# Experts' dot products on TensorE for every other tile, the gate product on GpSimd, filler products in the first chunk

## The chip, the cores and the metric

The kernel runs on one core of a Trainium2 chip. Its time is the device time of one execution in microseconds; the kernel before took 851.04 us (median of three runs, 850.98 to 857.43). TensorE multiplies matrices into PSUM; VectorE (DVE), ScalarE (ACT) and GpSimd (POOL) work on elements; SyncE (SP) issues nearly all transfers. Each engine works through its own queue in order and waits at semaphores for the others.

## The reference

Three layers in float32 follow each other.

```python
# 1. gated linear attention, 4 batches x 8 heads x 768 positions, head size 40, step by step:
m_new = maximum(f_gate[t] + m, i_gate[t])
f_stab, i_stab = exp(f_gate[t] + m - m_new), exp(i_gate[t] - m_new)
C = f_stab * C + i_stab * outer(v[t], k[t]);  n = f_stab * n + i_stab * k[t]
y[t] = sigmoid(o_gate[t]) * (C @ q[t]) / maximum(abs(n @ q[t]), 1)
# 2. on the 3072 rows of 320: h = x @ w_in (320 x 2048);  x = (h - tanh(h)) @ w_out
# 3. eight experts, one for each row:
logits = normalize(x) @ normalize(expert_emb).T / tau
e = argmax(logits);  gate = softmax(logits)[e]
out = gate * (relu(x @ w1[e]) @ w2[e])          # 320 -> 1024 -> 320
```

## The kernel before, in words

The 768 positions are cut into six **chunks** of 128; with four batches a chunk has four **units** (chunk `c`, batch `b`, unit `i = 4c + b`) of eight heads. Attention of a unit is made of pieces (in `attention`): `scores` (S: products of q and k into PSUM, exponentials on ScalarE, a mask on GpSimd), `weigh` (W: mask times scores on VectorE, and k times the last column of the mask), `outs` (O: on TensorE the state products `po`, the state's update `st`, and eight weighted sums `pi`, one for each head), `sums` (M: denominators, the **gate product** `z` = sigmoid times reciprocal, and the state `Cst`, scaled by the decay `eGL` and added to), `finish` (F: y = sum times z), `turn` (U: y transposed on TensorE) and `low` (L: the transposed rows as a high and a low part). From chunk 2 on q and k are split into high and low parts first (`parts`, Q).

The first layer's products (second in the reference) run in 96 **steps**, 16 for each chunk of 512 rows. A step is 8 TensorE products of 512 columns (`gemm1`, into `h`), a chain ScalarE, VectorE, ScalarE, GpSimd (`g_chain`, `g_split`) and 12 products of 320 columns (`gemm2`, into four `acc` banks). `gemm1` runs three steps ahead. While chunk `c` runs through its steps, the attention of chunk `c + 1` and the **routing** of chunk `c - 1` are woven in: `PLACE1` and `PLACE2` say at which step and position a piece stands, `ORDER` the positions within a step ('g' the special pieces and gemm2, 'r' one portion of routing, 'h' gemm1, the digits the attention pieces). In the first 16 steps the weights of this layer are prepared too (`prep`), and in chunk 5 the experts' weights begin.

Routing (`route`, `slots`) takes a chunk's result as four tiles of 128 rows, and makes for each tile the sums of squares and the eight dot products with the experts' normalized vectors. `VDOT[c]` says how many of the eight are made on VectorE (L263, a product with a running sum); the rest are a product on GpSimd (L267) and a sum on ScalarE (L268). Where `VDOT` is 0, as for chunk 5, `dots` makes them on TensorE: three transposes of the tile, two copies out of PSUM, three products with the transposed vectors `enT`, one copy of 8 columns. `enT` is made by `turn_en` at step 96 - 6 = 90. Then come exponentials, each row's place in its expert's list, and scatters to `xs`. Behind the 96 steps the experts' stage reads `xs` and runs 80 shorter steps.

What stands ahead of the bar in `START` (the **start**) runs in the order written there; chunk 0 has its attention there, in the letters above. What is traced after that is put in order by the framework's planner, which takes the traced order as priority and moves an instruction behind others when, by its own cost estimates, its inputs or its buffer come later. `at_bank` gives out PSUM banks; in the steps there are two of them for all of attention and routing, in turn.

`warm` issues filler products of 512 bf16 columns whose result nobody reads: `WARM0` = 20 at the very start, and two ahead of every scores piece of chunk 0.

Of the kernel before, what the change touches and what calls it, by code (L numbers as in the profile page):

```python
# [9 lines left out]
F32 = mybir.dt.float32  # L10
# [5 lines left out]
AF = mybir.ActivationFunctionType  # L16
ALU = mybir.AluOpType
# [5 lines left out]
NCH = S // L  # L23
# [4 lines left out]
E = 8  # L28
# [25 lines left out]
STACK = 12  # L54
SIGM = (2, 14)
EXPERT_X = (-3, 0)
LOAD_EW, LOAD_X, LOAD_X2, TURN_EN = 13, 4, 4, 6
KW_POOL = (0, 2, 3, 4, 5)
VDOT = (8, 8, 8, 8, 6, 0)
WARM0, WARM = 20, 2  # L60


BETA, GAMMA, C2 = -1.2788614, 4.7605257, 0.052115805
# [47 lines left out]
def build(ctx, tc, qk, qk3, vk, og, gat, w64, w12, emb, tau, cst, tok, empty, out):  # L111
    nc = tc.nc
    V, A, G, T = nc.vector, nc.scalar, nc.gpsimd, nc.tensor
    MM = T.matmul

    const = ctx.enter_context(tc.tile_pool(name="const", bufs=1))
# [105 lines left out]
    enT = []  # L222

    def turn_en():

        e8 = attp.tile([8, 320], F32, tag="z", name="e8", bufs=1)
        nc.sync.dma_start(out=e8, in_=es)
        pn = at_bank("pn")
        enT.append(attp.tile([128, 3, 8], F32, tag="dn", name="enT"))
        for k in range(3):  # L230
            n = min(128, 320 - 128 * k)
            T.transpose(pn[0:n, 8 * k:8 * k + 8], e8[:, 128 * k:128 * k + n], ident[0:8, 0:8])
            A.activation(out=enT[0][0:n, k, :], in_=pn[0:n, 8 * k:8 * k + 8], func=AF.Copy)

    def dots(x2, lg):

        pd = at_bank("pd")
        xt = attp.tile([128, 384], F32, tag="y", name="xt")
        for k in range(3):
            n = min(128, 320 - 128 * k)  # L240
            T.transpose(pd[0:n, 128 * k:128 * k + 128], x2[:, 128 * k:128 * k + n], ident)
        V.tensor_copy(out=xt[:, 0:256], in_=pd[:, 0:256])
        A.activation(out=xt[0:64, 256:384], in_=pd[0:64, 256:384], func=AF.Copy)
        for k in range(3):
            n = min(128, 320 - 128 * k)
            MM(pd[:, 384:392], xt[0:n, 128 * k:128 * k + 128], enT[0][0:n, k, :], start=k == 0, stop=k == 2)
        V.tensor_copy(out=lg, in_=pd[:, 384:392])

    def slots(pool, nj, R, si, vdot=E, part=E):

        n = nj * 8
# [3 lines left out]
        for j in range(nj):  # L255
            x2 = R[:, j, 0:320]
            A.activation(out=jk[0], in_=x2, func=AF.Square, accum_out=ss[:, j:j + 1])
            if vdot == 0:
                dots(x2, lg[:, j, :])
                yield  # L260
            for e in range(E if vdot else 0):
                if e < vdot:
                    V.scalar_tensor_tensor(out=jk[1], in0=x2, scalar=1.0, in1=enb[:, e, :], op0=ALU.mult, op1=ALU.mult,  # L263
                                           accum_out=lg[:, j, e:e + 1])
                else:
                    dt = attp.tile([128, 320], F32, tag="A", name="dt")
                    G.tensor_tensor(out=dt, in0=x2, in1=enb[:, e, :], op=ALU.mult)  # L267
                    A.activation(out=jk[0], in_=dt, func=AF.Copy, accum_out=lg[:, j, e:e + 1])  # L268
                if (e + 1) % part == 0:
                    yield  # L270
# [20 lines left out]
        for j in range(1, nj):  # L291
# [12 lines left out]
                        in1=col(C_EOFF, n).rearrange("p (j e) -> p j e", j=nj), op=ALU.add)  # L304
# [67 lines left out]
    attp = p1.enter_context(tc.tile_pool(name="attp", bufs=2))  # L372
# [3 lines left out]
    Cst = attp.tile([104, 16, 82], F32, tag="C", name="C", bufs=1)  # L376
    gts = {}
    units = {}
    sig = {}
# [3 lines left out]
    eGL = attp.tile([104, NCH * 16], F32, tag="eGL", name="eGL", bufs=1)  # L383
# [143 lines left out]
    def attention(c):  # L527
# [3 lines left out]
        def unit(b):  # L531
            i = c * B + b
# [50 lines left out]
            def outs():  # L583
                po = v['po'] = at_bank("po")
                st = po[:, 336:500].rearrange("p (j d) -> p j d", j=4)
                if i >= TWO:
                    for h in range(8):
                        MM(po[:, 42 * h:42 * h + 42], v['q', h % 2][0:120, h // 2 * L:(h // 2 + 1) * L],
                           C3[0][0:120, b, h % 2, h // 2, :], start=True, stop=True)
                elif c:  # L590
                    for j in range(4):
                        MM(po[:, 82 * j:82 * j + 82], qT[0:104, j, :], Cst[:, 4 * b + j, :], start=True, stop=True)
                if c + 1 < NCH:
                    for h in range(8):
                        p0 = 64 * (h % 2)
                        MM(st[p0:p0 + 40, h // 2, :], v['kw'][:, h, :], v1[:, h, :], start=True, stop=True)
                pi = v['pi'] = at_bank("pi")
                for h in range(8):
                    MM(pi[:, 41 * h:41 * h + 41], v['A', h % 2][:, h // 2, :], v1[:, h, :], start=True, stop=True)
                if i >= 4:  # L600
                    load_d(i + 2)
                if 4 <= i < TWO - 2:
                    load_unit(i + 2)
                elif 4 <= i < NCH * B - 2:
                    units[i + 2] = load_vk(i + 2)
                if TWO - 2 <= i < TWO:
                    load_half(i + TWO + 2)

            def sums():
# [5 lines left out]
                if c:  # L615
                    Tt = v['T'] = attp.tile([128, 8, 41], F32, tag="T", name="T", bufs=1)
                    V.tensor_tensor(out=tmp, in0=po[:, 0:w * 8].rearrange("p (h d) -> p h d", h=8)[:, :, 0:41],
                                    in1=eG[:, 8 * i:8 * i + 8].unsqueeze(2).to_broadcast([128, 8, 41]),
                                    op=ALU.mult)
                    V.tensor_tensor(out=Tt.rearrange("p h d -> p (h d)"), in0=pi[:, 0:328],  # L620
                                    in1=tmp.rearrange("p h d -> p (h d)"), op=ALU.add)
                else:
# [4 lines left out]
                V.tensor_tensor(out=dn, in0=nq, in1=dn, op=ALU.max)  # L627
                V.reciprocal(out=dn, in_=dn)
                z = v['z'] = attp.tile([128, 8, 40], F32, tag="z", name="z", bufs=1)
                (V if c > 1 else G).tensor_tensor(out=z, in0=sig[i].rearrange("p (h d) -> p h d", h=8),  # L630
                                                  in1=dn.to_broadcast([128, 8, 40]), op=ALU.mult)
                if c == 0:
                    for par in range(2):
                        p0, c0 = 64 * par, 41 * par
                        A.activation(out=Cst[p0:p0 + 40, 4 * b:4 * b + 4, c0:c0 + 41], in_=st[p0:p0 + 40, :, :],
                                     func=AF.Copy)
                for par in range(2 if 0 < c < NCH - 1 else 0):
                    p0, c0 = 64 * par, 41 * par
                    Cv = Cst[p0:p0 + 40, 4 * b:4 * b + 4, c0:c0 + 41]
                    V.tensor_tensor(out=Cv, in0=Cv, in1=eGL[p0:p0 + 40, 4 * i:4 * i + 4].unsqueeze(2)  # L640
                                    .to_broadcast([40, 4, 41]), op=ALU.mult)
                    V.tensor_tensor(out=Cv, in0=Cv, in1=st[p0:p0 + 40, :, :], op=ALU.add)
            def finish():
                y = v['y'] = attp.tile([128, 384], F32, tag="y", name="y")
# [139 lines left out]
    def warm(bank, n=None):  # L784
        for _ in range((WARM if c0[0] else 0) if n is None else n):
            MM(bank, oneb, busy, start=True, stop=True)
# [30 lines left out]
    NS = NCH * NF  # L817
# [136 lines left out]
            sp[n] = relu_chain(hs.pop(n), rows_of(step(n)[0])[3])  # L954

    def special(n, c, f, rx):
        if n == NS - TURN_EN:
            turn_en()
        if n == NS - NF - 4:
            ranking()  # L960
# [274 lines left out]
```

## Time and profile before

| | |
|---|---|
| median of three runs | 851.04 us (850.98 to 857.43) |
| profiled execution | 854.08 us, span 852.1 us |
| TensorE busy | 763.0 us (90%) |
| VectorE busy | 638.1 us (75%) |
| ScalarE busy | 496.1 us (58%) |
| GpSimd busy | 364.3 us (43%) |
| mean granted TensorE clock | 0.927 |

The span is that of one profiled execution, from its first to its last instruction. Busy time is the time in which an engine works on an instruction; TensorE's matmuls are pipelined and their ends are modelled, so that a busy TensorE is not one at its peak. The clock is the share of 2.4 GHz that was granted: 1.00 or, in some stretches, 0.50. A row's idle time and its releaser say how long the engine had nothing to do ahead of it and what came last. The first `gemm2` of each chunk marks the chunks: they begin at 73.4, 176.3, 275.5, 374.3, 463.8 and 545.7 us, and the experts' stage at 621.7.

### The profile page before, as it was taken

Reading aid. Unit: us, or ns where it says so; the run is one execution under the profiler, and the core shown is the slowest. Engines: PE = TensorE matmul, PEld = TensorE weight load, DVE = VectorE, ACT = ScalarE, POOL = GpSimd, SP = SyncE. Lnnn points to the kernel's source line nnn. Section 1 sums busy time; section 2 is a strip of 40 time slices with the busy share of each in tenths; the row PEclk is TensorE's granted clock in tenths of the full one; section 3 lists DMA queues with packets and bytes.
Section 4 is the critical chain, followed back from the end, with each engine's and each line's share of the span. In section 5 each row is a group of like instructions: output and inputs, shape, how many; then the busy total and the mean of one; then the engine's idle time right before and its main releaser. Section 6 shows DMA issues by size and latency. Waiting matters only on the chain. (4 is left out here: it accounts for less than half of the span.)

```text
span 852.1 us, 14301 instructions
## 1 busy us (share of the span) xinstructions
PE 763.0 (90%) x4640; PEld 677.6 (80%) x4640; DVE 638.1 (75%) x1417; ACT 496.1 (58%) x1175; POOL 364.3 (43%) x375
## 2 busy tenths in 40 slices
PE   8979899797899898998889989888899999999994
PEld 5767778686788687787778778767799989999994
DVE  6476999898887989879986999797473775556420
ACT  3775787767557645685558634655554655455421
POOL 2383677657463554655463525443522111012111
PEclk8558998988989989999999999999999999999998
DMA  8574766543344243432335311201535764455000
GB/s 273 211 254 160 257 220 198 133 122 93 87 126 131 82 101 87 143 105 79 89 109 152 92 34 44 73 1 51 177 115 164 232 181 140 120 173 165 36 20 21
DMA packets 60756, 107.55 MB, mean 126 GB/s; under 512 B 24958, under 2 KB 33321, under 8 KB 60016
## 3 DMA queue, kind: packets, MB, share of 16 engines
q1 hardware_dynamic: 57968, 98.46, 38.8%
q0 software_dynamic: 2512, 7.89, 2.5%
q8 instruction: 38, 0.62, 0.3%
q14 instruction: 46, 0.38, 0.1%
q10 hardware_dynamic: 192, 0.20, 0.1%
HBM read 92.91 MB, written 17.87 MB: 130 GB/s over the span
## 5 line engine op out<-in xcount | busy, mean ns | idle before, releaser
L185 PE MATMUL h<-xh,wi 128*128 128x512 f32 (+6 forms) x880 | 303.3, 382 | 18.8 <-DVE g L213 13.3
L185 PEld LDWEIGHTS h<-xh,wi 128*128 128x128 f32 x880 | 171.7, 198 | 45.7 <-DVE g L213 17.3
L193 PE MATMUL acc<-wo,ghi 128*128 128x320 f32 (+1 forms) x616 | 200.6, 326 | 0.0
L162 POOL TENSOR_TENSOR glo<-g,ghi 128x512 fp32r<-128x512 f32 x96 | 133.2, 1389 | 156.6 <-ACT ghi L218 119.8
L185 PE MATMUL h<-xl,wi 128*128 128x512 f32 (+6 forms) x528 | 197.7, 379 | 0.4
L195 PE MATMUL acc<-wo,glo 128*128 128x320 f32 (+1 forms) x616 | 194.9, 317 | 2.0 <-POOL glo L162 2.0
L194 PE MATMUL acc<-wo,ghi 128*128 128x320 f32 (+1 forms) x616 | 194.7, 316 | 0.0
L218 ACT ACTIVATE ghi<-g 128x512 fp32r<-128x512 f32 x96 | 60.2, 628 | 111.7 <-DVE g L213 94.6
L193 PEld LDWEIGHTS acc<-wo,ghi 128*128 128x128 f32 (+1 forms) x616 | 118.4, 192 | 6.1 <-ACT D L568 1.3
L195 PEld LDWEIGHTS acc<-wo,glo 128*128 128x128 f32 (+1 forms) x616 | 117.7, 191 | 4.0 <-POOL glo L162 3.2
L194 PEld LDWEIGHTS acc<-wo,ghi 128*128 128x128 f32 (+1 forms) x616 | 118.1, 192 | 3.2
L185 PEld LDWEIGHTS h<-xl,wi 128*128 128x128 f32 x528 | 105.0, 199 | 12.3 <-DVE xl L660 1.6
L212 DVE SCALAR_TENSOR_TENSOR s<-s,u 128x512 f32<-128x512 f32 x96 | 78.9, 822 | 41.8 <-ACT s L211 40.2
L263 DVE SCALAR_TENSOR_TENSOR jk<-R,enb 128x320 bf16<-128x320 f32 x152 | 96.5, 635 | 2.7 <-ACT R L727 1.7
L156 POOL DMA_INDIRECT out<-ob,ti x29 | 28.5, 982 | 156.9 <-ACT ob L1053 133.3
L929 DVE SCALAR_TENSOR_TENSOR glo<-h,ghi 128x256 fp32r<-128x256 f32 (+5 forms) x80 | 41.4, 517 | 60.0 <-ACT ghi L928 54.5
L568 ACT ACTIVATE D<-D,bcol 128x128 f32<-128x128 f32 x192 | 64.6, 390 | 33.6 <-DMA D<-gd 33.3
L928 ACT ACTIVATE ghi<-h 128x256 fp32r<-128x256 f32 (+5 forms) x80 | 36.7, 458 | 65.4 <-PE acc L194 55.9
L162 DVE TENSOR_TENSOR wi<-ew,wi 128x256 fp32r<-128x256 f32 (+1 forms) x128 | 50.1, 392 | 31.4 <-ACT wi L174 29.8
L211 ACT ACTIVATE s<-u,cs 128x512 f32<-128x512 f32 x96 | 68.7, 716 | 0.9
L213 DVE SCALAR_TENSOR_TENSOR g<-s,h 128x512 f32<-128x512 f32 x96 | 65.4, 682 | 2.9
L210 ACT ACTIVATE u<-h 128x512 f32<-128x512 f32 x96 | 55.9, 583 | 12.6 <-PE h L185 11.3
(192 smaller groups left out, 1199.5 us busy)
## 6 DMA issues: line engine op xcount, KB each, us to landing
ew<-in_w SPq DMA_DIRECT2D x64, 352.0 KB
W<-in_qk SPq DMA_DIRECT2D x32, 480.0 KB
D<-gd SPq DMA_DIRECT2D x48, 256.0 KB
raw<-in_w SPq DMA_DIRECT2D x16, 704.0 KB
vk<-in_vk SPq DMA_DIRECT2D x20, 324.0 KB
xs<-blank SPq DMA_DIRECT2D x32, 161.0 KB
sg<-in_og SPq DMA_DIRECT2D x6, 640.0 KB
ys<-y SPq DMA_DIRECT2D x24, 160.0 KB
```

The lines of the kernel that those rows point to most:

```text
L162: eng.tensor_tensor(out=out, in0=x, in1=hi.bitcast(F32), op=ALU.subtract)
L185: MM(h[:, 0:cols], wi[:, k, :], x[:, kk, :], start=n == 0, stop=n == len(seq) - 1)
L193: MM(o, ghi[:, sl], wo[:, 0, 0:320], start=first, stop=False)
L194: MM(o, ghi[:, sl], wo[:, 1, 0:320], start=False, stop=False)
L195: MM(o, glo[:, sl], wo[:, 0, 0:320], start=False, stop=last)
L210: A.activation(out=u, in_=h, func=AF.Square, accum_out=usum[:, n:n + 1])
L211: A.activation(out=s, in_=u, func=AF.Square, bias=col(C_BETA))
L212: V.scalar_tensor_tensor(out=s, in0=s, scalar=GAMMA, in1=u, op0=ALU.add, op1=ALU.mult)
L213: V.scalar_tensor_tensor(out=g, in0=s, scalar=C2, in1=h, op0=ALU.mult, op1=ALU.mult)
L218: A.activation(out=ghi, in_=g, func=AF.Copy)
L263: V.scalar_tensor_tensor(out=jk[1], in0=x2, scalar=1.0, in1=enb[:, e, :], op0=ALU.mult, op1=ALU.mult, accum_out=lg[:, j, e:e + 1])
L568: A.activation(out=Dt[:, j, :], in_=Dt[:, j, :], func=AF.Exp, bias=bcol[:, k:k + 1])
```

## The change

- `slots`: in the routing of chunks 0 to 4, tiles 0 and 2 now take the path through `dots`, tiles 1 and 3 make all eight products on VectorE (`VDOT` 8 in place of 6 for chunk 4). Each `dots` tile is one portion of routing, each VectorE tile two.
- `dots`: the wide copy out of PSUM is on ScalarE.
- `turn_en` runs at step 12, and `enT` has a tile of its own.
- `outs`: in chunk 0 one filler stands ahead of each of the eight weighted sums of a unit, 32 in all. `WARM0` is 26.
- `sums`: the gate product is on GpSimd in every chunk (before, on VectorE from chunk 2 on). The decay of the state is one product over 104 partitions and 4 x 82 columns instead of two over 40 partitions and 4 x 41.

```diff
--- before.py
+++ after.py
@@ -54,10 +54,10 @@
 STACK = 12
 SIGM = (2, 14)
 EXPERT_X = (-3, 0)
-LOAD_EW, LOAD_X, LOAD_X2, TURN_EN = 13, 4, 4, 6
+LOAD_EW, LOAD_X, LOAD_X2, TURN_EN = 13, 4, 4, 12
 KW_POOL = (0, 2, 3, 4, 5)
-VDOT = (8, 8, 8, 8, 6, 0)
-WARM0, WARM = 20, 2
+VDOT = (8, 8, 8, 8, 8, 0)
+WARM0, WARM = 26, 2
 
 
 BETA, GAMMA, C2 = -1.2788614, 4.7605257, 0.052115805
@@ -226,7 +226,7 @@
         e8 = attp.tile([8, 320], F32, tag="z", name="e8", bufs=1)
         nc.sync.dma_start(out=e8, in_=es)
         pn = at_bank("pn")
-        enT.append(attp.tile([128, 3, 8], F32, tag="dn", name="enT"))
+        enT.append(const.tile([128, 3, 8], F32, tag="enT", name="enT"))
         for k in range(3):
             n = min(128, 320 - 128 * k)
             T.transpose(pn[0:n, 8 * k:8 * k + 8], e8[:, 128 * k:128 * k + n], ident[0:8, 0:8])
@@ -239,7 +239,7 @@
         for k in range(3):
             n = min(128, 320 - 128 * k)
             T.transpose(pd[0:n, 128 * k:128 * k + 128], x2[:, 128 * k:128 * k + n], ident)
-        V.tensor_copy(out=xt[:, 0:256], in_=pd[:, 0:256])
+        A.activation(out=xt[:, 0:256], in_=pd[:, 0:256], func=AF.Copy)
         A.activation(out=xt[0:64, 256:384], in_=pd[0:64, 256:384], func=AF.Copy)
         for k in range(3):
             n = min(128, 320 - 128 * k)
@@ -255,10 +255,11 @@
         for j in range(nj):
             x2 = R[:, j, 0:320]
             A.activation(out=jk[0], in_=x2, func=AF.Square, accum_out=ss[:, j:j + 1])
-            if vdot == 0:
+            on_pe = vdot == 0 or part < E and j % 2 == 0
+            if on_pe:
                 dots(x2, lg[:, j, :])
                 yield
-            for e in range(E if vdot else 0):
+            for e in range(0 if on_pe else E):
                 if e < vdot:
                     V.scalar_tensor_tensor(out=jk[1], in0=x2, scalar=1.0, in1=enb[:, e, :], op0=ALU.mult, op1=ALU.mult,
                                            accum_out=lg[:, j, e:e + 1])
@@ -596,6 +597,8 @@
                         MM(st[p0:p0 + 40, h // 2, :], v['kw'][:, h, :], v1[:, h, :], start=True, stop=True)
                 pi = v['pi'] = at_bank("pi")
                 for h in range(8):
+                    if c == 0:
+                        warm(idle, 1)
                     MM(pi[:, 41 * h:41 * h + 41], v['A', h % 2][:, h // 2, :], v1[:, h, :], start=True, stop=True)
                 if i >= 4:
                     load_d(i + 2)
@@ -627,18 +630,19 @@
                 V.tensor_tensor(out=dn, in0=nq, in1=dn, op=ALU.max)
                 V.reciprocal(out=dn, in_=dn)
                 z = v['z'] = attp.tile([128, 8, 40], F32, tag="z", name="z", bufs=1)
-                (V if c > 1 else G).tensor_tensor(out=z, in0=sig[i].rearrange("p (h d) -> p h d", h=8),
+                G.tensor_tensor(out=z, in0=sig[i].rearrange("p (h d) -> p h d", h=8),
                                                   in1=dn.to_broadcast([128, 8, 40]), op=ALU.mult)
                 if c == 0:
                     for par in range(2):
                         p0, c0 = 64 * par, 41 * par
                         A.activation(out=Cst[p0:p0 + 40, 4 * b:4 * b + 4, c0:c0 + 41], in_=st[p0:p0 + 40, :, :],
                                      func=AF.Copy)
+                if 0 < c < NCH - 1:
+                    Cu = Cst[:, 4 * b:4 * b + 4, :]
+                    V.tensor_tensor(out=Cu, in0=Cu, in1=eGL[:, 4 * i:4 * i + 4].unsqueeze(2).to_broadcast([104, 4, 82]), op=ALU.mult)
                 for par in range(2 if 0 < c < NCH - 1 else 0):
                     p0, c0 = 64 * par, 41 * par
                     Cv = Cst[p0:p0 + 40, 4 * b:4 * b + 4, c0:c0 + 41]
-                    V.tensor_tensor(out=Cv, in0=Cv, in1=eGL[p0:p0 + 40, 4 * i:4 * i + 4].unsqueeze(2)
-                                    .to_broadcast([40, 4, 41]), op=ALU.mult)
                     V.tensor_tensor(out=Cv, in0=Cv, in1=st[p0:p0 + 40, :, :], op=ALU.add)
             def finish():
                 y = v['y'] = attp.tile([128, 384], F32, tag="y", name="y")
@@ -954,7 +958,7 @@
             sp[n] = relu_chain(hs.pop(n), rows_of(step(n)[0])[3])
 
     def special(n, c, f, rx):
-        if n == NS - TURN_EN:
+        if n == TURN_EN:
             turn_en()
         if n == NS - NF - 4:
             ranking()
```

## Rows read from the trace of the kernel before

**Rows 1.** The page: granted TensorE clock in 40 slices of the span, in tenths.
```profile
PEclk8558998988989989999999999999999999999998
```
**Rows 2.** Windows, one a chunk: stretch, length, busy PE, PEld, DVE, ACT, POOL; clock.
```profile
73.40:176.30 102.90, 91.04 (x563) 79.44 (x562) 93.29 (x144) 73.69 (x168) 69.85 (x70) 0.91 0.57 181
176.30:275.50 99.20, 85.67 (x528) 75.71 (x527) 81.39 (x187) 62.02 (x149) 54.20 (x52) 0.91 0.44 119
275.50:374.30 98.80, 86.40 (x527) 76.14 (x526) 86.45 (x201) 61.19 (x143) 51.98 (x51) 0.91 0.37 100
374.30:463.80 89.50, 80.19 (x511) 70.24 (x510) 79.71 (x174) 57.96 (x136) 46.23 (x45) 0.98 0.40 111
463.80:545.70 81.90, 73.45 (x432) 63.73 (x431) 74.27 (x184) 44.67 (x107) 36.00 (x29) 1.00 0.22 68
545.70:621.70 76.00, 64.30 (x339) 54.84 (x339) 59.64 (x142) 46.19 (x122) 33.67 (x31) 0.96 0.22 69
```
**Rows 3.** TensorE's waits in chunk 1 (176 to 275 us): total, times, longest.
```profile
PE ps L564 <- DVE q L162: 9.3, 2, 5.3
```
**Rows 4.** Windows of three single steps: without attention, with weighted sums, in chunk 4.
```profile
482.10:485.80 3.70, 3.70 (x23) 3.33 (x23) 3.70 (x10) 2.29 (x4) 1.92 (x2) 1.00 0.34 90
362.30:369.10 6.80, 6.80 (x62) 6.32 (x60) 2.18 (x5) 6.77 (x14) 2.57 (x2) 1.00 0.39 94
518.90:525.20 6.30, 6.30 (x47) 5.93 (x46) 4.98 (x12) 3.42 (x8) 3.56 (x3) 1.00 0.08 29
```
**Rows 5.** Groups by line and shape: count, busy us, mean ns, idle before.
```profile
L263 DVE SCALAR_TENSOR_TENSOR jk<-R,enb 128x320 bf16<-128x320 f32 x152 | 96.5, 635 | 2.7 <-ACT R L727 1.7
...
L640 DVE TENSOR_TENSOR C<-C,eGL 40x164 f32<-40x164 f32 x32 | 17.3, 540 | 5.8 <-PE po L592 4.7 <-POOL Cl L162 0.6
...
L630 DVE TENSOR_TENSOR z<-sg,dn 128x320 f32<-128x320 f32 x16 | 12.7, 795 | 0.2
```
**Rows 6.** Timeline of TensorE in the last chunk's dots: start, length, instruction, count.
```profile
621.15 0.81 PE L241 MATMUL pd<-cs,R 128*128 128x128 f32 x6
...
622.84 0.93 PE L246 MATMUL pd<-enT,xt 128*128 128x8 f32 x6
```
**Rows 7.** Instructions on the tile pd: shortest, median, longest ns; first and last start.
```profile
L242 DVE COPY xt<-pd x4: 414/415/424, 621.7 to 626.1; 128x256 f32<-128x256 f32 x4
L243 ACT ACTIVATE xt<-pd x4: 266/270/271, 622.5 to 626.6; 64x128 f32<-64x128 f32 x4
```
**Rows 8.** Timeline, chunk 4: one small VectorE operation and the GpSimd products beside it.
```profile
527.26 2.89 DVE L627 TENSOR_TENSOR dn<-T,dn 128x8 f32<-128x8 f32 x1
...
527.56 2.56 POOL L162 TENSOR_TENSOR glo<-g,ghi 128x512 fp32r<-128x512 f32 x2
```
**Rows 9.** Timeline of TensorE in the start; in brackets idle time and releaser.
```profile
13.95 1.82 PE L562 MATMUL ps<-ue 40*128 40x128 f32 x8 [1.18 <-DMA ue<-in_qk]
...
20.58 3.64 PE L599 MATMUL pi<-ue,A 128*128 128x41 f32 x16
24.01 1.05 PE L786 MATMUL ps<-busy,oneb 128*128 128x512 bf16 x2
25.00 2.07 PE L562 MATMUL ps<-ue 40*128 40x128 f32 x8
...
41.56 0.77 PE L596 MATMUL po<-ue,kw 128*40 128x41 f32 x14 [0.30 <-POOL kw L578]
...
55.97 0.66 PE L653 MATMUL px<-cs,y 128*128 128x128 f32 x2 [4.25 <-DVE y L645]
...
67.30 1.86 PE L599 MATMUL pi<-vk,A 128*128 128x41 f32 x14
```
**Rows 10.** Window of the stretch that holds the dots of chunk 4's tiles.
```profile
544.00:575.00 31.00, 24.80 (x122) 20.61 (x120) 30.61 (x72) 19.80 (x59) 16.62 (x15) 0.94 0.00 1
```
**Rows 11.** Waits of the whole execution: GpSimd's mask for ScalarE's exponential.
```profile
POOL D L569 <- ACT D L568: 45.2, 23, 9.8
```
**Rows 12.** TensorE's waits in chunk 0 (73 to 176 us).
```profile
PE px L653 <- DVE y L645: 4.7, 2, 2.7
```

## Prediction

> **What bounds it now.** I read the page's busy shares and clock line first, then busy time chunk by chunk, then who TensorE waits for, then single rows. TensorE's clock is at half speed through much of the first 64 us and near full from there [rows 1]; the expert stage behind 621.7 us is touched by no part of the change. So the question is the start (to 73.4 us) and the six chunks of 16 steps each, 548.3 us together. In the chunks TensorE is busy for 481 us and VectorE for 475, the six rows added up [rows 2]: two engines, each nearly full, and neither covers the other. Who is the waiter? In chunk 1 TensorE's longest waits are for VectorE, its split of q above all [rows 3].
>
> What would TensorE need alone? A step with nothing beside the two products takes 3.7 us, one with a unit's weighted sums 6.8, and 6.3 in chunk 4, whose last units have no state product; TensorE is busy throughout and at full clock in all three [rows 4]. So 16 x 3.7 + 4 x 3.1 = 71.6 us is the floor of a chunk (69.6 in chunk 4); scores and transposes, alike in chunks 1 to 4, are left in what lies above. Above it stand 27.6 us in chunk 1, 27.2 in chunk 2, 17.9 in chunk 3, 12.3 in chunk 4. Chunk 4 carries the same products with the dots of chunk 3 on VectorE, but less state work. Its 12.3 us is the least excess that this schedule has shown, so I take it as what stays. Chunks 1 and 2 can then give back about 15 us each, chunk 3 5.6.
>
> **Part by part.** *Dots.* For chunks 0 to 3, 16 of the 32 dot products (two tiles of eight) leave VectorE; at 0.635 us [rows 5] that is 10.2 us a chunk, spent in the steps of the next chunk. For chunk 4 24 become 16: 5.1 us, and GpSimd's eight products with their eight sums on ScalarE go too. In their place comes, per tile, what the last chunk does already: three transposes, two copies, three products (each shows as two), a copy of 8 columns. Six transposes (two tiles) lasted 0.81 us and six product rows (one tile) 0.93 [rows 6]: at most 0.4 + 0.9 = 1.3 us of TensorE a tile, 2.6 a chunk, 13 over ten tiles. The wide copy moves from VectorE (0.415) to ScalarE, beside the narrow one of 0.27 [rows 7], so some 0.7 us a tile on an engine that is busy for 45 to 62 us in chunks 1 to 5 [rows 2]: nothing. If that cover fails, the products wait on TensorE with the next product of the chunk queued behind them; the rows show 0.88 us between the end of the transposes (621.96) and the first product (622.84), filled with other products. Uncovered it is 10 x 0.9 = 9 us; I take 0.
>
> *Gate product.* 16 products move from VectorE (0.795 each, 12.7 in all) to GpSimd [rows 5], four in each of chunks 1 to 4: 3.2 us a chunk. But VectorE and GpSimd hinder each other: an operation on 128 x 8 elements lasted 2.89 us while two GpSimd products ran for 2.56 [rows 8]. So the relief is between 0 and 3.2 a chunk; nearest is the mixed mean of all those rows, and I take half, 1.6.
> The Trainium skill's SBUF — State Buffer, "Who interferes with whom", says that a VectorE instruction with two SBUF inputs and a GpSimd one that reads SBUF lock each other out for a whole instruction, and by that rule the move would be worth the low end, nothing, 3.2 us less over chunks 1 and 2.
>
> *State decay.* Two products of 164 columns (0.540 each) become one of 328. Not seen before: between one half (0.54) and both (1.08); nearest is the gate product, 320 columns from SBUF, 0.795 [rows 5]. That saves 0.3 a unit, 1.1 us in each of chunks 0 to 3.
>
> *Experts' vectors turned at step 12 instead of 90*, in a tile of their own: three transposes, three copies and a small load on SP's queue move from chunk 5 into chunk 0, where TensorE idles 11.9 us [rows 2]. Nothing. The load needs the single buffer of the gate product, so loads behind it on SP could slip by a step, 6.4 us (102.9 / 16), once; I take 0. The new score banks and the turned tiles use buffers that attention uses (two each): 0 again, with the 9 us above as bound.
>
> *Fillers.* Unit 0's 16 sum products at half clock last 3.64 us; at full clock 14 of them last 1.86, so 2.1 for 16 [rows 9]. A pair of fillers takes 0.99 at half clock (24.01 to 25.00): eight are 4.0 us a unit, 2.0 at full. If the clock stays at half, four units add 16 us, less the 0.30 that TensorE waits at 41.56. If it rises in the first unit, each unit is 4.1 long, 0.5 more than now, and each scores piece (2.07 at half) loses about 1, but units 2 and 3 still wait for GpSimd at 41.56: about -1 in all. Between these no row decides: half-speed stretches there hold two fillers in some 3 us, and none holds eight. I take a rise with the second unit: 4.0 + 3 x 0.5 - 2 x 1.0 - 0.3 = +3. All of it reaches the end of the start, since the last unit's turn waited 4.25 us for VectorE behind these sums. The six extra fillers at the very start last at most 6 x 0.5 = 3.0, in part inside the 1.18 us that TensorE waited for a load at 13.95 [rows 9], and the first sums wait for GpSimd anyway: 0, at most 1.8.
>
> **The sum.** VectorE is relieved by 10.2 + 1.6 + 1.1 = 12.9 us in each of chunks 1 to 3. Chunks 1 and 2: 12.9 is below the 15 they can give, less 2.6 of TensorE: 10.3 each. Chunk 3: 5.6 - 2.6 = 3.0. Chunk 4: it is its own yardstick, 0. Chunk 5: its first 31 us hold the dots, and VectorE is busy for 30.6 of them [rows 10]: 5.1 - 2.6 = 2.5. Chunk 0: 1.1. Together 27.2, less 3 for the start: 24. The profiled execution took 854.08 us (span 852.1 and 2.0 outside it): 830. The median of the three runs is 3.04 lower: **827 us**.
>
> Bounds: all of the gate product's relief gives 3 more; at full clock instead of 0.91, TensorE's 172 us in chunks 1 and 2 would shrink by up to 15, since it was fewer waits, not less work, that chunk 4 had at clock 1.00; so some 809. The other way, 9 us of uncovered dots, 13 more of fillers: 849.
>
> **Rivals.**
> *A, VectorE was not what held the chunks.* For it: chunk 5 has the least VectorE work (59.6 of 76 us) and the highest idle share of TensorE, 11.7 of 76 [rows 2]; the chain of one step through ScalarE, VectorE and GpSimd waits for itself. Against it: 6.2 of that idle time lies in the 31 us of dots [rows 10], and chunks 2 and 4 rank in excess as in VectorE's load. Then dots only fill TensorE's holes, gains and costs cancel: 851 - 1 + 3 = 853, down to 843 if half remains. Chance 0.19.
> *B, the gate product comes late on GpSimd (slower).* GpSimd works in order and waits, 23 times, 2.0 us on average for a ScalarE exponential ahead of its masks, at worst 9.8 [rows 11]. A gate product queued behind that holds y, then y's transposes on TensorE, then every product behind. In chunk 0, where it is on GpSimd today, the transposes waited 4.7 us for y [rows 12], 1.2 a unit. At that price 16 units cost 19 us: 846. At 2.0 and its own 0.8 each they cost 45: 872. It turns the sign from 1.5 us a unit on. Against: the planner may put it ahead of the masks. Chance of slower by this 0.13.
> *C, fillers at half clock throughout:* +15.7 in place of +3: 840. For it: the two fillers per scores piece did not hold the clock. Chance 0.17.
> The forecast itself has 0.51.
>
> **Numbers.** A measurement here tells about 1% from no change. Faster by over 1% (below 842.5): forecast 0.51, C 0.15, a little of A 0.03: 0.69. Within: A 0.16, C 0.02: 0.18. Slower: B, 0.13. Leaving out B's long side and the best end, the range is 806 to 850.
>
> **What would show it.** Dots: 80 VectorE rows in place of 152, and VectorE's busy time in chunks 1 to 3 lower by some 13 us each; the chunks near 89, 88, 86, 82, 73 us. Rival A: VectorE much less busy with chunk lengths as now, and waits for ScalarE or GpSimd in the place of waits for q and k. B: transposes of y waiting, y waiting for the gate product. Fillers: the clock between 20 and 51 us, and where the first second product starts (73.4 now): 76 by the forecast, 89 in C. The forecast is wrong if chunks 1 and 2 do not each lose at least 5 us, or lose it without VectorE's waits shrinking.

## The result and the profile after

The changed kernel took **861.09 us** (median of eight runs, 854.78 to 863.55), the kernel before beside it 851.83 (849.38 to 857.43): a ratio of 1.0082 [1.0059, 1.0105]. By the ratio it is slower by 7.0 us (the two medians lie 9.3 apart), less than the 1% that was called no change. It lies above the forecast of 827 us and its range, which ended at 850. The profiled execution of the changed kernel took 861.92 us, span 860.2, mean granted clock 0.928; below, ratios are turned into us at 852. Two of the ten runs of `dots_only` below are in a slower state and are left out of its ratio, which therefore lies below that of the medians; all other runs count.

The clock line of the page, as [rows 1] show it for before, and the windows of the start and of the six chunks, the chunks as in [rows 2] (columns: stretch, length, busy PE, PEld, DVE, ACT, POOL, clock, DMA share, GB/s).

```profile
PEclk8878998889999989999969889999899999999998
```
```profile
0.00:75.20 75.20, 59.62 (x355) 44.19 (x361) 45.68 (x89) 44.85 (x109) 34.85 (x51) 0.81 0.70 237
75.20:180.40 105.20, 92.55 (x569) 79.68 (x568) 89.65 (x143) 76.55 (x180) 69.46 (x70) 0.91 0.56 180
180.40:277.00 96.60, 86.44 (x547) 77.01 (x545) 65.86 (x147) 62.15 (x147) 56.01 (x58) 0.93 0.45 120
277.00:371.70 94.70, 85.04 (x548) 75.82 (x545) 64.88 (x148) 59.08 (x140) 49.80 (x51) 0.95 0.39 104
371.70:471.70 100.00, 87.97 (x529) 78.42 (x528) 68.71 (x159) 62.54 (x149) 50.02 (x52) 0.90 0.38 103
471.70:555.40 83.70, 80.20 (x451) 71.96 (x450) 59.20 (x142) 45.02 (x108) 35.68 (x31) 0.92 0.21 62
555.40:630.30 74.90, 65.19 (x353) 57.40 (x352) 53.73 (x129) 43.47 (x109) 26.36 (x24) 0.93 0.23 70
```

VectorE's relief came: it is busy for 65.9, 64.9 and 68.7 us in chunks 1 to 3 where it was busy for 81.4, 86.5 and 79.7 [rows 2], 563.3 us in the whole span against 638.1. The time did not follow. Against before the start is 1.8 us longer, chunk 0 2.3, chunk 1 2.6 shorter, chunk 2 4.1 shorter, chunk 3 **10.5 longer**, chunk 4 1.8 longer, chunk 5 1.1 shorter; the experts' stage lasts 229.9 against 230.4. And the clock line has a 6 in its 21st slice (430 to 452 us), where that of before stands at 9 [rows 1].

The groups by line that answer to [rows 5] (count, busy us, mean ns, idle before and its releaser): 80 dots in place of 152, the joined decay, and the gate product now on GpSimd.

```profile
L264 DVE SCALAR_TENSOR_TENSOR jk<-R,enb 128x320 bf16<-128x320 f32 x80 | 49.8, 622 | 0.8
L642 DVE TENSOR_TENSOR C<-C,eGL 104x328 f32<-104x328 f32 x16 | 10.8, 675 | 7.0 <-PE po L593 4.7 <-POOL Cl L162 2.3
```
```profile
L633 POOL TENSOR_TENSOR z<-sg,dn 128x320 f32<-128x320 f32 x24 | 20.5, 856 | 21.9 <-DVE dn L631 20.3 <-PE acc L195 1.0
```

What does VectorE wait for? Two lines of its waits in the whole execution (total us, times, longest); below them the one line of before that answers to the second. The first has no counterpart before.

```profile
DVE R L732 <- DMA xs<-R,si: 24.3, 4, 7.0
DVE y L649 <- POOL z L633: 15.8, 16, 3.3
```
```profile
DVE y L645 <- POOL z L630: 1.8, 3, 0.6
```

L732 is a copy of four columns, `R[:, :, 321]`, the token numbers of a chunk's rows, from a constant. It opens the routing of chunk `c`, needs nothing but a free buffer `R`, and its result is needed only when that chunk ends. `R` shares its two buffers (L729) with a state copy that keeps one of them (L506), so in the changed kernel the buffer is the one from which the scatters of chunk `c - 1` still read. In the kernel before, the copy never waited: in chunks 1 to 3 it ran at 258.20, 355.57 and 447.65, 7 to 8 us after the last scatter had started (250.20, 348.07, 440.25). The first of these pairs:

```profile
250.20 0.97 POOL L156 DMA_INDIRECT xs<-R,si  x1 [0.30 <-issue]
258.20 0.17 DVE L728 COPY R<-cs 128x4 f32<-128x4 f32 x1
```

In chunk 4 of before it ran at 524.07, between two scatters and without a wait, so there it cannot have had their buffer. With the dots done earlier the scatters come earlier (the last of chunk 0 starts 58.4 us into chunk 1 in place of 73.9), and VectorE reaches the copy while they are still being issued; why the planner sets it there was not tested. The worst of the four waits, in VectorE's timeline (start, length, instruction, idle time before and releaser), the last scatter in GpSimd's, and TensorE's:

```profile
426.94 0.72 DVE L162 TENSOR_TENSOR k<-W,k 40x512 fp32r<-40x512 f32 x1
434.67 0.17 DVE L732 COPY R<-cs 128x4 f32<-128x4 f32 x1 [7.01 <-DMA xs<-R,si]
434.75 0.55 DVE L664 TENSOR_TENSOR xl<-px,xh 128x384 fp32r<-128x384 f32 x1
435.22 1.39 DVE L212 SCALAR_TENSOR_TENSOR s<-s,u 128x512 f32<-128x512 f32 x1
436.64 0.69 DVE L213 SCALAR_TENSOR_TENSOR g<-s,h 128x512 f32<-128x512 f32 x1
```
```profile
429.50 0.97 POOL L156 DMA_INDIRECT xs<-R,si  x1 [0.30 <-issue]
```
```profile
433.23 0.31 PE L195 MATMUL acc<-wo,glo 128*128 128x320 f32 x1
437.39 0.80 PE L185 MATMUL h<-xh,wi 128*128 128x512 f32 x1 [3.84 <-DVE g L213]
```

VectorE had reached the copy at 427.66, before the fourth scatter was even issued, and stood there until the scatters had landed; behind it in its queue lay the chain of the next step (L212, L213), and TensorE waited for that chain. Then the clock was at half for 17 us:

```profile
435.53:452.60 17.07, 15.21 (x66) 13.85 (x67) 8.24 (x16) 7.16 (x17) 5.93 (x7) 0.50 0.15 39
```

Relief and loss stand side by side in four steps of chunk 1 of the changed kernel: the first holds the dots of a tile, the second and third correspond to the two longest steps of before, the fourth holds the copy and the scatters. Below them stand the two longest steps of before, in which VectorE was busy nearly throughout.

```profile
180.40:190.20 9.80, 6.61 (x34) 5.71 (x32) 7.99 (x18) 5.45 (x16) 9.02 (x9) 0.80 0.91 223
207.60:211.90 4.30, 4.30 (x27) 3.85 (x26) 3.56 (x11) 1.85 (x5) 2.55 (x3) 1.00 0.62 163
228.90:233.40 4.50, 4.50 (x31) 3.92 (x30) 3.21 (x9) 2.47 (x5) 3.18 (x3) 1.00 0.22 38
238.80:250.40 11.60, 7.28 (x62) 6.32 (x60) 4.10 (x8) 5.16 (x14) 6.08 (x6) 1.00 0.35 112
```
```profile
199.30:211.40 12.10, 6.81 (x29) 5.70 (x27) 11.91 (x34) 7.28 (x19) 7.51 (x8) 0.75 0.03 6
226.90:237.00 10.10, 6.11 (x29) 5.20 (x27) 9.94 (x22) 4.48 (x10) 4.08 (x7) 0.83 0.24 59
```

The same four steps of before lasted 4.3, 12.1, 10.1 and 6.9 us. So 13.4 us are won in the two that VectorE had held, and 10.2 go in the two others. How much of the fourth is the copy's, these rows do not say; experiment 1 does.

### The profile page after: what moved, and what is told of

Its sections match the earlier page's. It is cut to its first block, busy times and chain, and to the rows that moved or that the text cites. A ratio compares the mean times of both kernels' runs of the same rounds, so it can differ in the third digit from the quotient of the medians.

```text
span 860.2 us, 14421 instructions
## 1 busy us (share of the span) xinstructions
PE 772.2 (90%) x4763; PEld 692.8 (81%) x4768; DVE 563.3 (65%) x1247; ACT 499.6 (58%) x1183; POOL 358.9 (42%) x383
## 5 line engine op out<-in xcount | busy, mean ns | idle before, releaser
L195 PEld LDWEIGHTS acc<-wo,glo 128*128 128x128 f32 (+1 forms) x616 | 118.7, 193 | 12.8 <-POOL glo L162 12.2
L218 ACT ACTIVATE ghi<-g 128x512 fp32r<-128x512 f32 x96 | 60.2, 628 | 107.4 <-DVE g L213 87.9
L212 DVE SCALAR_TENSOR_TENSOR s<-s,u 128x512 f32<-128x512 f32 x96 | 78.3, 815 | 63.5 <-ACT s L211 63.1
L185 PEld LDWEIGHTS h<-xl,wi 128*128 128x128 f32 x528 | 105.3, 199 | 11.6 <-DVE xl L664 1.2
L213 DVE SCALAR_TENSOR_TENSOR g<-s,h 128x512 f32<-128x512 f32 x96 | 65.5, 683 | 2.9
L570 POOL TENSOR_SCALAR_AFFINE_SELECT D<-D 128x512 f32<-128x512 f32 x48 | 35.3, 736 | 63.8 <-ACT D L569 63.3
```

What stands on the lines that cost most here:

```text
L185: MM(h[:, 0:cols], wi[:, k, :], x[:, kk, :], start=n == 0, stop=n == len(seq) - 1)
L195: MM(o, glo[:, sl], wo[:, 0, 0:320], start=False, stop=last)
L212: V.scalar_tensor_tensor(out=s, in0=s, scalar=GAMMA, in1=u, op0=ALU.add, op1=ALU.mult)
L213: V.scalar_tensor_tensor(out=g, in0=s, scalar=C2, in1=h, op0=ALU.mult, op1=ALU.mult)
L218: A.activation(out=ghi, in_=g, func=AF.Copy)
```

## The experiments

**1. The copy set late.** The token write is made to depend on the chunk's own result, so that the planner cannot put it ahead of it. `late` is the changed kernel with this edit, `late_before` the kernel before with it, the control.

```diff
-        V.tensor_copy(out=R[:, :, 321], in_=cs[:, C_TOK + c * B:C_TOK + c * B + NJ])
+        V.scalar_tensor_tensor(out=R[:, :, 321], in0=R[:, :, 0], scalar=0.0, in1=cs[:, C_TOK + c * B:C_TOK + c * B + NJ],
+                               op0=ALU.mult, op1=ALU.add)
```

> The changed kernel, with the token numbers of a chunk written into R by an operation that also reads R's data (0 x R + tokens), so that VectorE cannot come to it before the chunk's result is there. Theory T (VectorE's queue stands still at that copy until the last chunk's scatters have landed, 24.3 us over four chunks, and TensorE's chain and its clock with it): VectorE's waits for the scatters gone, steps 26, 42 and 58 near 5 us instead of 11.6, 11.6 and 16.7, about 15 to 20 us less than the changed kernel's 861: 841 to 846. Rival P (the dots' own waits on TensorE, 12.4 us, and the clock they cost): those stay, 856 to 861. Rival Z (the gate product on GpSimd): no difference, 858 to 861.

> The kernel before with the same late token write: the control. In it VectorE never waited for a scatter at that copy, so theory T and both rivals expect no difference: 849 to 854. If it is faster by over 5 us, the late write does something else than take that wait away.

`late`: 843.72 us against 853.22, ratio 0.9881 [0.9849, 0.9914], 0.0201 or **17 us** below the change as it is, as theory T had it. VectorE's waits in it no longer name the scatters; the one for the gate product is still there:

```profile
DVE y L649 <- POOL z L633: 14.8, 16, 1.8
```

Rival P falls: TensorE's waits for the dots are as long in `late` as in the change (12.8 and 12.4 us). But theory T did not have all of it right. The steps with the scatters, 26, 42 and 58, were to come down to 5 us; they last 10.9, 8.9 and 8.3, where the change has 11.6, 11.6 and 16.6. With step 74, the fourth that holds the copy (7.6 to 6.8 us), and step 59, which ran at half clock in the change (6.3 to 3.7), they give 15.1 of the 17 us, 10.9 of it in steps 58 and 59; in the other steps gains and losses of up to 6 us cancel. In step 26 next to nothing is won. `late` in that step, in a window, then in GpSimd's and TensorE's timelines:

```profile
239.60:250.50 10.90, 8.52 (x61) 7.73 (x59) 4.16 (x7) 7.42 (x19) 7.87 (x8) 0.84 0.36 121
```
```profile
240.14 0.98 POOL L156 DMA_INDIRECT xs<-R,si  x1 [0.30 <-issue]
241.12 1.29 POOL L162 TENSOR_TENSOR glo<-g,ghi 128x512 fp32r<-128x512 f32 x1
```
```profile
242.47 0.64 PE L195 MATMUL acc<-wo,glo 128*128 128x320 f32 x1 [2.38 <-POOL glo L162]
```

The step's `glo`, the low part that `gemm2` needs, stands in GpSimd's queue behind the four scatters, which were issued from 235.63 to 241.12, and TensorE waits for it. That wait is left when the copy's is gone.

`late_before`: 857.55 us, 1.0060 [1.0029, 1.0091], above the 849 to 854 that was expected; the edit is no gain in itself, rather a cost of 5 us whose cause stays open. So the copy's early place costs the changed kernel 17 us, and the loss exists only where the routing is done early.

**2. The gate product.** `z_back` is the changed kernel with the gate product on VectorE from chunk 2 on, as before; `z_only` is the kernel before with it on GpSimd everywhere.

```diff
-                G.tensor_tensor(out=z, in0=sig[i].rearrange("p (h d) -> p h d", h=8),
+                (V if c > 1 else G).tensor_tensor(out=z, in0=sig[i].rearrange("p (h d) -> p h d", h=8),
```

> The changed kernel with the gate product on VectorE again from chunk 2 on. Rival Z: VectorE's waits of y for the gate product (15.8 us) and what they hold on TensorE go: 848 to 855. Theory T and rival P: little moves, 857 to 863.

> The kernel before with only the gate product on GpSimd in all chunks. Theory Z (the detour costs by itself: y stands in VectorE's queue and waits for GpSimd): 856 to 863, VectorE waiting 10 to 16 us for the gate product. Rival (it costs only where GpSimd and VectorE already stand still behind the scatters, as in the changed kernel): 850 to 854. The forecast's term was 1.6 us less a chunk: 845 to 848.

`z_back`: 848.13 us, 0.9938 [0.9909, 0.9966], 12 us below the change, with the wait for the scatters still there (23.6 us, 4 times). `z_only`: 861.62, 1.0104 [1.0074, 1.0133], 9 us above before. The move is a loss alone and within the change, by the size that rival Z and theory Z had set down. Two views of `z_only` say how: VectorE's waits, and the page's busy line.

```profile
DVE y L645 <- POOL z L630: 9.0, 14, 1.2
```
```profile
PE 759.0 (88%) x4640; PEld 675.5 (79%) x4640; DVE 637.6 (74%) x1401; ACT 493.3 (57%) x1175; POOL 376.5 (44%) x391
```

VectorE gave away 16 products that had taken 12.7 us [rows 5] and is busy for 637.6 us against 638.1: its other instructions together took 12.2 us longer. On top, it now stands before `y` until GpSimd has made `z`, 14 times, 0.64 us on average (before: 3 times, 1.8 us in all), and everything behind `y` in its queue stands too.

**3. The dots.** `dots_back` is the changed kernel with all dots back on VectorE and GpSimd; `dots_only` is the kernel before with the dots of tiles 0 and 2 on TensorE and the early turn, without the other parts.

```diff
 # dots_back
-            on_pe = vdot == 0 or part < E and j % 2 == 0
+            on_pe = vdot == 0
-VDOT = (8, 8, 8, 8, 8, 0)
+VDOT = (8, 8, 8, 8, 6, 0)
```

> The changed kernel with all dot products where they were (VectorE, and GpSimd for two of chunk 4's); gate product, decay, fillers and the early turn of the experts' vectors as changed. Theory T: the token copy stands two steps behind the scatters again, as in the kernel before, so its wait goes, and so does VectorE's relief: near the kernel before, 846 to 853. Rival P: the same range. If it stays at 858 or more, dots and token copy are both innocent, and the start, the gate product or the decay carries the loss.

> The kernel before with only the dots of tiles 0 and 2 on TensorE (and the early turn of the experts' vectors that they need). VectorE is relieved, but the token copy stands one step behind the scatters. Theory T: as the kernel with the gate product moved back, 845 to 851, with some 24 us of waits for scatters. The forecast's term for the dots alone was 24 us: 829. Rival P (the dots' waits on TensorE eat all): 853 or more.

`dots_back`: 856.11 us, 1.0047 [1.0022, 1.0072]; the wait for the scatters is gone, and the dots' load on VectorE is back. It is above the 846 to 853 that was expected: the gate product, the fillers and the decay, which it keeps, come to +7.8 us by their single runs (8.9, 2.5 and -3.6), the measured 4.0 being within their uncertainty. `dots_only`: 856.98, 0.9994 [0.9959, 1.0029]. The dots alone bring nothing; that is rival P's range and not theory T's. VectorE's waits in `dots_only` show the copy at work:

```profile
DVE R L729 <- DMA xs<-R,si: 25.1, 4, 8.0
```

This run alone does not decide between the copy and P. `late_z_fill` below does: it has the same dots, with 7.8 us of waits for them on TensorE against 10.8 here, and is 20 us faster, 3.6 of them by the decay.

**4. Both hindrances away.** `late_z` has the edits of `late` and `z_back` together; `late_z_fill` drops the fillers too (`WARM0` 20, none between the sums). What is left of the change in it is dots (with their copies on ScalarE), decay and early turn.

> The changed kernel with both: token numbers written late, gate product on VectorE from chunk 2 on. Theory T+Z (two separate losses, the token copy's wait and the gate product's detour over GpSimd, 17 and 13 us in the runs so far): they add up in part, 831 to 838. Rival O (one loss seen twice: both only shift the same stretches behind the scatters): 841 to 847.

> The same without the fillers between the weighted sums and with 20 at the start. If the fillers pay as little as the start says (the first second product comes at 75.2 to 75.6 us with them, at 73.4 to 74.0 without): 1 to 3 us less than with them, 829 to 836. If their clock pays later: 1 to 3 us more.

`late_z`: 833.93 us against 853.46, 0.9769 [0.9730, 0.9809]; the two losses, 17.1 and 12.3 us alone, come to 26.7 together, so they are separate, as theory T+Z had it. `late_z_fill`: **831.85**, 0.9756 [0.9725, 0.9786]. The token write of chunk 3 now comes 32 us after the last scatter of chunk 2 has started (417.24), and waits for nothing:

```profile
449.24 0.15 DVE L730 SCALAR_TENSOR_TENSOR R<-R,cs 128x4 f32<-128x4 f32 x1
```

Its six chunks:

```profile
74.70:180.80 106.10, 92.69 (x569) 79.30 (x568) 91.64 (x146) 77.04 (x181) 70.91 (x71) 0.92 0.58 183
180.80:268.70 87.90, 82.74 (x546) 74.29 (x545) 67.23 (x144) 61.15 (x145) 50.37 (x52) 0.96 0.46 125
268.70:359.20 90.50, 83.90 (x547) 74.19 (x546) 69.57 (x159) 60.56 (x145) 48.54 (x50) 0.96 0.41 109
359.20:450.00 90.80, 85.30 (x530) 77.04 (x529) 68.09 (x158) 61.70 (x145) 45.77 (x45) 0.92 0.41 113
450.00:530.60 80.60, 76.90 (x452) 69.10 (x450) 60.82 (x145) 45.51 (x108) 33.37 (x27) 0.94 0.21 65
530.60:604.80 74.20, 65.92 (x352) 58.71 (x351) 54.99 (x130) 43.51 (x108) 25.92 (x24) 0.91 0.22 71
```

VectorE is as relieved as in the changed kernel (67.2, 69.6, 68.1 us in chunks 1 to 3), and now chunks 1 and 2 are shorter by 11.3 and 8.3 us: VectorE's work was what held them. Chunk 3 is 1.3 us longer than before and chunk 0 3.2.

**5. Fillers and decay alone.** `fill_only` and `decay_only` are the kernel before with that part alone.

```diff
 # fill_only
                 for h in range(8):
+                    if c == 0:
+                        warm(idle, 1)
-WARM0, WARM = 20, 2
+WARM0, WARM = 26, 2
```

> The kernel before with the fillers alone: a pair of idle products between the sixteen sums of chunk 0's units and 26 instead of 20 at the start. The forecast priced them at +3 us (range -1 to +16). Theory F (they cost time that TensorE has to spare): the start, 73.4 us before, ends between 74 and 76, and the ratio is 1.000 to 1.004; late_z with and without them differed by 2 us. If it is above 1.008, the fillers alone would make up the whole loss of the change. Chunk 0, 102.9 us before, 105.2 after the change: if it is 105 here, the fillers are why; if it is 103, it is the early turn or the dots.

> The kernel before with the two decay products of 164 columns joined into one of 328, in front of the loop over the halves. The forecast took 0.3 us of VectorE a unit, 1.1 us a chunk in chunks 1 to 4. Theory P (price right): the joined product lasts 0.75 to 0.85 us against 1.08 for both, and the time falls by 0 to 4 us, ratio 0.995 to 1.000. Rival: the joined product has to wait for the last reader of both halves and sits ahead of the first half's work in VectorE's queue, so VectorE stands in front of it; then a wait of VectorE at that line and a ratio over 1.002.

`fill_only`: 857.36 us against 855.76, 1.0029 [1.0003, 1.0056], 2.5 us above. The start is 74.6 us long against 73.4, chunk 0 102.7 against 102.9. The clock did rise behind the first unit's fillers; its windows and a row of TensorE's timeline show where that went:

```profile
26.00:39.40 13.40, 10.03 (x84) 7.54 (x82) 4.33 (x10) 7.46 (x16) 3.25 (x5) 1.00 0.51 167
39.40:46.00 6.60, 4.38 (x29) 3.43 (x30) 5.74 (x13) 6.48 (x19) 6.06 (x8) 0.50 0.47 128
```
```profile
39.38 0.87 PE L655 MATMUL px<-cs,y 128*128 128x128 f32 x3 [3.37 <-DVE y L647]
```

From 26.0 us TensorE ran at full clock, waited 3.37 us for VectorE's `y`, and was back at half from 39.4.

`decay_only`: 852.10 us, 0.9958 [0.9932, 0.9983], 3.6 us below. The joined product (groups by line, `decay_only`):

```profile
L639 DVE TENSOR_TENSOR C<-C,eGL 104x328 f32<-104x328 f32 x16 | 14.8, 924 | 4.1 <-PE po L592 3.2 <-POOL Cl L162 0.9
```

Sixteen products take 14.8 us where 32 took 17.3 [rows 5]. One lasts 0.92 us on average, above the 0.75 to 0.85 that was expected (0.675 in the change); the time gained is of the forecast's size all the same. The rival, a wait at that line with a ratio over 1.002, falls: 4.1 us of idle time stand before it, but 5.8 stood before the halves.

**6. What is left.** `best_vcopy` is `late_z_fill` with both copies of the turned tile on VectorE; `turn5` is `late_z_fill` with the experts' vectors turned at step 5.

```diff
 # best_vcopy
-        A.activation(out=xt[:, 0:256], in_=pd[:, 0:256], func=AF.Copy)
-        A.activation(out=xt[0:64, 256:384], in_=pd[0:64, 256:384], func=AF.Copy)
+        V.tensor_copy(out=xt[:, 0:256], in_=pd[:, 0:256])
+        V.tensor_copy(out=xt[0:64, 256:384], in_=pd[0:64, 256:384])
 # turn5
-LOAD_EW, LOAD_X, LOAD_X2, TURN_EN = 13, 4, 4, 12
+LOAD_EW, LOAD_X, LOAD_X2, TURN_EN = 13, 4, 4, 5
```

> late_z_fill (after the change, with the token write tied to the data, the gate product back on VectorE, no fillers; 0.9756) with both copies of the turned tile on VectorE instead of ScalarE. In late_z_fill the dots' products waited 4.1 us in chunks for ScalarE's second copy, whose queue held exponentials that wait for their loads. Theory S (ScalarE's queue is that wait): the products no longer wait for ScalarE, and the time falls by 2 to 5 us, ratio 0.970 to 0.974. Rival (VectorE is the fuller engine, 20 copies of 0.25 to 0.4 us, 7 us in all, go on top of it and the wait turns to VectorE): ratio 0.975 to 0.985.

> late_z_fill with the experts' vectors turned at step 5 in place of step 12 of chunk 0. Chunk 0 lasted 106.1 us in late_z_fill against 102.9 before. Theory T (the turn at step 12 falls in with the last weighted sums and the routing of the first tiles and costs those 3 us): chunk 0 is back at 103, ratio 0.971 to 0.974. Rival (it is the dots on TensorE at steps 15 and 16 themselves that lengthen chunk 0, where it was to lose only 1.1): chunk 0 stays at 105 to 107, ratio 0.974 to 0.978.

`best_vcopy`: 833.71 us against 855.76, 0.9728 [0.9687, 0.9769]. That is in theory S's range, but against `late_z_fill` it is no difference that the intervals support. The products' wait for ScalarE's copy (4.1 us in the chunks) went, and one for VectorE's came, as the rival had it, in TensorE's waits:

```profile
PE pd L246 <- DVE xt L243: 10.9, 6, 3.0
```

So either queue delays the copies, and no effect on the time is shown. `turn5`: 839.53, 0.9774 [0.9715, 0.9834]: no gain, and chunk 0 is 105.3 us long, much as with the turn at step 12 (106.1). That the turn comes at step 12 is not why chunk 0 is longer. That remains open: `dots_only` has the longest chunk 0, 109.6 us, but `dots_back`, without the dots, still has 105.0.

## Why the prediction was wrong

Its terms, beside what the runs showed (us against before; differences of ratios at 852, each uncertain by 2 to 5 us):

| part | forecast | measured | by |
|---|---|---|---|
| dots and decay, chunks 0 to 5 | -24 | -21 | `late_z_fill` |
| of it decay | -3.3 | -3.6 | `decay_only` |
| fillers | +3 | +1 to +2.5 | `late_z` less `late_z_fill`; `fill_only` |
| gate product | -3 | +9 to +12 | `z_only`, `late` less `late_z`, the change less `z_back` |
| token copy before the scatters | none | +14 to +17 | `z_back` less `late_z`, the change less `late` |

The forecast column is the prediction's sum taken apart: of its 27.2 us, the gate product had 1.6 in each of chunks 1 and 2, the decay 1.1 in each of chunks 0 to 2, the dots the rest. In chunks 1 and 2 the changed kernel lost 2.6 and 4.1 us, less than the 5 each that the prediction had set as the sign of being wrong. From `late_z_fill` over `late_z` and `late` to the change the ratios make a chain: -20.8, +1.1, +9.5, +17.1, together +6.9.

**The step that failed first** is the one that costed the dots: it took the 10.2 us off VectorE chunk by chunk and left all else in place. It did not ask what the routing's earlier end sets free. The prediction named the queue that the turn's load passes and the buffers that the dots share with attention, but not that `R` has one of two buffers, that a copy without inputs waits for it, and that an indirect transfer reads it. An instruction of 0.17 us took 24.3 us of VectorE's time, and 14 to 17 of the kernel's.

**The gate product** failed as the second step: "I take half, 1.6". The row that spoke for the low end was there, 2.89 us for a small operation beside two GpSimd products [rows 8]. In `z_only` VectorE's busy time moved by 0.5 us where 12.7 us of work had left. The Trainium skill's SBUF — State Buffer, "Who interferes with whom", says that a VectorE instruction with two SBUF inputs contends with a GpSimd one that reads SBUF; the nothing that the prediction worked out from it agrees with those 0.5 us, but no run shows that this is their reason. And zero was not the low end. The prediction had "the relief is between 0 and 3.2 a chunk" and left the detour to rival B. B's price, 1.2 us a unit, was read from TensorE's wait for `y` in chunk 0 [rows 12], not from VectorE's wait for the gate product, which is 1.2 us there for all four units. The loss of 9 to 12 us is 0.6 to 0.75 a unit, about half of B's price, with 14 waits of 0.64 us in `z_only` and 16 of 0.99 in the change. Its place was half right: the transposes of `y` did not wait more in the chunks (0.6 us between 180 and 472); VectorE itself stood. That what lay behind `y` was late for it is argued from the order of the queue, not shown row by row. B forecast a slower kernel, and it is slower, but B would have needed 24 us for that; the copy, which no rival named, made up the rest.

**The main argument held in chunks 1 and 2.** "16 x 3.7 + 4 x 3.1" and chunk 4's excess as what stays gave 89, 88, 86, 82 and 73 us for chunks 1 to 5; `late_z_fill` has 87.9, 90.5, 90.8, 80.6 and 74.2, and 106.1 for chunk 0 where 101.8 was forecast. Chunks 0 and 3 are the ones that missed. Chunk 3 was to give 3.0 and is 1.3 longer than before, at a clock of 0.92 where it was 0.98 [rows 2]. What the forecast had no term for is the longest of TensorE's waits in these chunks:

```profile
PE acc L195 <- POOL glo L162: 10.5, 7, 2.4
```

Before it was 1.5 us. Four of the seven, 8.6 us, come behind the scatters of a chunk in GpSimd's queue, as in step 26 of `late`. The early scatters thus also hold up GpSimd; what that costs was not tested.

**Uncovered dots** ("Uncovered it is 10 x 0.9 = 9 us; I take 0") cost something. TensorE's waits in the changed kernel:

```profile
PE pd L246 <- ACT xt L243: 8.0, 4, 3.2
PE pd L241 <- DVE T L623: 4.4, 2, 3.2
```

The cover that was named, ScalarE's busy 45 to 62 us a chunk, is a mean; the copy stood behind an exponential that waited for its load. ScalarE's and TensorE's timelines at the largest:

```profile
186.38 0.40 ACT L569 ACTIVATE D<-D,bcol 128x128 f32<-128x128 f32 x1 [2.45 <-DMA D<-gd]
186.68 0.36 ACT L242 ACTIVATE xt<-pd 128x256 f32<-128x256 f32 x1
186.95 0.26 ACT L243 ACTIVATE xt<-pd 64x128 f32<-64x128 f32 x1
```
```profile
187.26 1.54 PE L246 MATMUL pd<-enT,xt 128*128 128x8 f32 x6 [3.19 <-ACT xt L243]
```

The second wait is for a bank, since both of attention's banks are shared, which was also taken at 0. Together they are 12.4 us, 3.4 over the prediction's bound of 9. In `late_z_fill` 7.8 are left; whether they are among the 3 us by which dots and decay fell short is not shown.

**Fillers.** The clock rose with the first unit, not the second, and the start got no shorter: part of what TensorE won it waited for `y`. That +3 is near the measured +1 to +2.5 is in part luck. Of the row of 1.86 us that was read as full clock [rows 9], the window 67.30 to 69.16 says 0.91; this changes the sum by less than 1 us.

**Rival A** would have looked true from the changed kernel's page alone: VectorE much less busy, the chunks together much as long as before, waits for other things. `late_z_fill` disproves it for chunks 1 and 2. Rival C did not happen: the start's clock is 0.81 in the change. The range began at 806, below the 809 that the prediction's own bounds come to; nothing hangs on it.

## What to carry to other kernels

When work is taken off an engine, list what the engine will reach sooner, above all instructions with no inputs that only wait for a buffer, and ask who still reads that buffer; here the indirect transfers held it until 3 to 5 us after the last of them had started. Ask also what the work that now comes earlier will stand in front of, as the scatters do on GpSimd. In an in-order queue a write of 0.17 us can stop everything behind it, and tying it to data that comes late kept the planner from placing it there. Where a moved operation's result goes back to the engine it left, price the return trip, not only the relief.

## What had not been expected of the hardware

After a stop of 3.84 us TensorE had its clock at half for 17.07 us, though it was busy for 15.21 of them; the kernel before has no half-speed stretch longer than 6.8 us in its chunks, and neither has `z_back`, though the wait for the scatters is in it. Sixteen weighted sums in that stretch:

```profile
443.33 3.64 PE L602 MATMUL pi<-vk,A 128*128 128x41 f32 x16
```

At full clock sixteen take 1.98 us (`late`, at 248.74). If all of the stretch's work scaled like that, 15.21 us would have been 8.3: an estimate of some 7 us lost behind a stop of 3.84. The copy's price does not need such a stretch: without one, `z_back` less `late_z` is 14 us. VectorE's dots of the same shape lasted 622 ns on average against 635, so taking half of them away did not speed up the others.
